# Last batches' routing and loop end in another order, operands of the experts' order in PSUM, conversions in two parts over two steps

## The chip, the cores and the metric

The kernel runs on one core of one Trainium2 chip. The metric is the device time of one execution in microseconds. Three runs of the kernel before took 1173.43, 1176.47 and 1177.87 us, median 1176.47 us.

## The reference, cut to what matters

Three stages follow each other, all in float32: linear attention without a softmax and with a norm per head, a layer of eight experts with a skip, and a gated layer.

```python
# q, k, v: 8 batches, 8 heads, 576 tokens, 64 numbers
kv = einsum('bhsd,bhse->bhde', k, v)
out = einsum('bhsd,bhde->bhse', q, kv)
x = out / sqrt(mean(out * out, -1) + 1e-6) * g_norm      # then 4608 tokens of 512 numbers
...
do_compute = x @ w_skip > 0
e_idx = argmax(x[do_compute] @ w_gate); gate_w = softmax(...)[e_idx]
for e in range(8):                                       # w1 512 x 1024, w2 1024 x 512
    y[mask] = gate_w[mask] * (relu(xc[mask] @ w1[e]) @ w2[e])
x[do_compute] = xc + y
...
h = x @ w_in                                             # 512 x 2048
out = (h * sigmoid(h)) @ w_out                           # 2048 x 512
```

## The kernel before, in words

**Attention** (loop over batches b = 0 to 7 and steps u within each; a batch with odd b has a fifth step for 64 tokens of each of two batches). In every step `attend` multiplies q with the state of two heads' groups into a PSUM tile of the pool `ps_o` (two buffers), ScalarE squares and copies it out into `rows_b[b]`, and VectorE sums the squares (L473, L494). The state of a batch comes from `kv_heads` (k times v, four parts), `kv_copy` (ScalarE) and `kv_state` (two parts, which make the weights `wt`, copied by ScalarE at L450). The dictionary `KV` says in which step which part of which batch's state is made; parts 0 to 3 are `kv_heads`, 4 and 5 are `kv_state`. `early` puts a step's `attend` ahead of the state's parts. `keep_busy` multiplies a unit matrix into a PSUM tile that nobody reads, so that TensorE does not idle.

A pair of batches is then routed: `norm` (the inverse root of the mean square, ScalarE and VectorE), `scale` (GpSimd multiplies the rows, once by g_norm, `grow`, once by the norm, `inv`, at L607), `logits`, `choose`, `count`, `weigh`, `marked`, `ranks` (TensorE, each token's rank within its expert), `own_rank`, `places` and `fill` (TensorE, L783: the lists of tokens of each expert, in the PSUM tile `slots`). `weave` lets several such chains take turns, one VectorE operation at a time. `order_experts` sorts the experts by the number of their tokens in all batches but the last, from the totals `pc` of `sT`; `order_slots` takes the capacities and bases of the sorted experts. SP reads the order into registers (`load_experts`, L559) and issues the loads of the first expert weights.

`store` (SP, L623 and L630) writes a batch's finished rows to the DRAM tile `xs`; `STORES` says in which step. At the end `count` (L1021) is loaded into a register of every engine, and a loop follows that handles experts with more tokens than their capacity; here its count is zero. `gsel` and `gidx` (L959, L964) are the lists sorted by expert. `fetch(0)` gathers the first expert's rows (GpSimd, L967).

Each engine takes its instructions in the order of the program, SP and GpSimd their DMAs too.

**Experts** (steps n = 0 to 63; step n is part f = n % 8 of expert u = n // 8). In a step `first` makes 12 matmuls (L1303), ScalarE and VectorE make the hidden values h and their rest (L1309, L1310), and `second` of the step before makes 9 or 6 (L1355). float32 is multiplied as three products of a rounded part and a rest. So every weight chunk is split: an expert's chunk by ScalarE and VectorE (L187, L188), once a step. A chunk of the gated layer's weights arrives as pairs of integers and is converted by `split`, half a chunk at a time: ScalarE takes the low word (L197), VectorE the high word in five operations (L198 to L210), and later `split_on`, called in every step, has ScalarE write the rounded part (L221), GpSimd multiply and subtract (L222, L223), and, a step later, VectorE add (L218). `at_step` says in which step which conversion is made: 22 in the expert stage, at steps 2, 4 and 6 of each expert and the last at step 55; ten more follow from step 64 on, four operations a step (`split_slowly`).

At an expert's end VectorE adds its result to the rows (L1365, three times), which are stored; `turn` transposes the next expert's rows (TensorE L1204 into a pool `ps_t` of two PSUM tiles, ScalarE L1215, VectorE L1216).

**Gated layer** (from step 64): three groups of 512 tokens in 16 steps each, then six more in pairs.

## Time and profile before

| | us |
|---|---|
| three runs: median (lowest to highest) | 1176.47 (1173.43 to 1177.87) |
| the profiled execution, its own time | 1185.35 |
| its span in the profile | 1183.3 |
| TensorE matmul busy | 1131.6 (96%) |
| TensorE weight load busy | 939.5 (79%) |
| VectorE busy | 595.2 (50%) |
| ScalarE busy | 484.0 (41%) |
| GpSimd busy | 368.8 (31%) |

In the profile PE is TensorE's matmul, PEld its weight load, DVE VectorE, ACT ScalarE, POOL GpSimd and SP the queue that issues most DMAs. Times are from the start of the span. PEclk is the granted TensorE clock as a share of 2.4 GHz. Attention lies in the first 122 us, the experts from about 141 to 405 us, the gated layer behind. "<-" names what ended an idle time; "issue" means that the profile shows nothing that the engine waited for.

### The profile page before, as it was taken

The page shows a single profiled execution, that of the slowest core. Times are in us where ns is not written, and L with a number is a line of the kernel's source. Part 1 is how long each engine was busy: PE and PEld are TensorE (multiplying, and loading weights), DVE is VectorE, ACT ScalarE, POOL GpSimd, SP SyncE. Part 2 cuts the span into 40 slices and gives each one's busy share as a digit, 9 for nine tenths or more (in the row PEclk, how much of TensorE's full clock was granted, in tenths as well). Part 3 has the DMA queues.
Part 4 walks back from the last instruction along what each step waited for, and adds up shares of the span by engine and source line. Part 5 has one row for each costly group of instructions (what it writes and reads, how often), then busy time and mean ns, then how long its engine had stood idle before and what let it go on. Part 6 is the DMA issues. An engine that isn't in the chain of part 4 may idle for free.

```text
span 1183.3 us, 16638 instructions
## 1 busy us (share of the span) xinstructions
PE 1131.6 (96%) x6259; PEld 939.5 (79%) x6259; DVE 595.2 (50%) x1105; ACT 484.0 (41%) x951; POOL 368.8 (31%) x369
## 2 busy tenths in 40 slices
PE   8895699999998999989999999999999999999998
PEld 7785698888886888868878788888888888888886
DVE  2467677788888577624535522355222453223222
ACT  3575354445444443422423444433244432344221
POOL 3679344535444186150063234120043200000000
PEclk9897799999999999999999999999999999999999
DMA  9867656666665433094641376432566322654202
GB/s 341 329 259 296 222 166 210 223 218 210 224 209 200 161 108 115 14 309 155 208 143 54 127 265 216 176 124 91 182 219 221 141 107 104 217 189 170 104 36 71
DMA packets 65265, 211.05 MB, mean 178 GB/s; under 512 B 9840, under 2 KB 24688, under 8 KB 53024
## 3 DMA queue, kind: packets, MB, share of 16 engines
q1 hardware_dynamic: 55760, 189.44, 45.8%
q0 software_dynamic: 8064, 20.48, 5.9%
q8 instruction: 50, 0.82, 0.3%
q10 hardware_dynamic: 1360, 0.05, 0.1%
q14 instruction: 31, 0.25, 0.1%
HBM read 162.67 MB, written 47.27 MB: 177 GB/s over the span
## 4 chain that ended last, share of the span: by engine, by line
PE 87%; DVE 5%; issue 3%; DMA 2%; ACT 2%; POOL 1%; SPq 0%; POOLq 0%; DVEq 0%; ACTq 0%
PE acc L1498 22%; PE acc L1355 19%; PE ph L1303 19%; PE pa L1451 11%; PE pc L1451 6%; PE pb L1451 3%; PE po L456 2%; PE kv L424 1%; PE pt L1204 1%; DVE w L188 1%; POOL x L223 1%; PE kv L426 1%; PE busy L1120 1%; PE G L445 0%; DMA xs<-rows 0%
## 5 line engine op out<-in xcount | busy, mean ns | idle before, releaser
L1355 PE MATMUL acc<-w,h 128*128 128x512 f32 x1128 | 282.4, 397 | 10.7 <-issue 5.5
L1303 PE MATMUL ph<-xT,w 128*128 128x512 f32 (+7 forms) x1344 | 265.8, 347 | 0.8 <-DVE w L188 0.4
L1498 PE MATMUL acc<-entry,h 128*128 128x512 f32 x1152 | 265.1, 392 | 0.0
L1498 PEld LDWEIGHTS acc<-entry,h 128*128 128x128 f32 x1152 | 216.3, 188 | 47.9
L1355 PEld LDWEIGHTS acc<-w,h 128*128 128x128 f32 x1128 | 203.4, 183 | 60.8 <-issue 7.5
L1303 PEld LDWEIGHTS ph<-xT,w 128*128 128x128 f32 x1344 | 225.3, 189 | 30.8 <-DVE w L188 0.7
L1001 POOL DMA_INDIRECT x<-xs,qidx x128 | 128.2, 1002 | 112.8 <-DVE room L1266 48.8
L1451 PE MATMUL pa<-b,entry 128*128 128x512 f32 x576 | 141.8, 393 | 0.0
L1479 DVE TENSOR_TENSOR h<-g,h 128x512 fp32r<-128x512 f32 x96 | 66.5, 693 | 147.8 <-ACT h L1478 145.4
L1451 PEld LDWEIGHTS pa<-b,entry 128*128 128x128 f32 x576 | 108.2, 188 | 24.8
L1478 ACT ACTIVATE h<-g 128x512 fp32r<-128x512 f32 x96 | 60.5, 630 | 146.6 <-PE acc L1498 141.5
L1317 DVE TENSOR_TENSOR h<-sg,h 128x512 fp32r<-128x512 f32 x48 | 34.8, 726 | 119.4 <-ACT h L1316 81.0
L188 DVE TENSOR_TENSOR w<-stg_None,w 128x1024 fp32r<-128x1024 f32 x64 | 80.3, 1256 | 17.3 <-ACT w L187 15.7
L1433 ACT ACTIVATE g<-g 128x512 f32<-128x512 f32 x72 | 45.4, 633 | 103.1 <-DVE g L1431 91.0
L1315 ACT ACTIVATE sg<-ph 128x512 f32<-128x512 f32 x48 | 28.7, 597 | 141.7 <-PE ph L1303 102.4
L222 POOL TENSOR_TENSOR x<-x,x 128x512 f32<-128x512 f32 x32 | 41.6, 1299 | 111.3 <-DVE x L210 106.1
L1451 PE MATMUL pc<-b,entry 128*128 128x512 f32 x288 | 74.3, 393 | 0.0
L1309 ACT ACTIVATE h<-ph 128x304 fp32r<-128x304 f32 (+6 forms) x64 | 28.0, 437 | 109.0 <-PE ph L1303 97.1
L187 ACT ACTIVATE w<-stg_None 128x1024 fp32r<-128x1024 f32 x64 | 67.1, 1049 | 9.8 <-DMA xs<-rows 9.8
L1451 PEld LDWEIGHTS pc<-b,entry 128*128 128x128 f32 x288 | 54.1, 188 | 12.4
L223 POOL TENSOR_TENSOR x<-x,w 128x512 f32<-128x512 f32 x32 | 62.9, 1966 | 0.6 <-ACT w L221 0.6
L1431 DVE TENSOR_TENSOR g<-pc,u 128x512 f32<-128x512 f32 x24 | 16.6, 692 | 73.0 <-PE pc L1451 73.0
(216 smaller groups left out, 1166.8 us busy)
## 6 DMA issues: line engine op xcount, KB each, us to landing
entry<-wa SPq DMA_DIRECT2D x42, 1024.0 KB
stg_None<-in_we_dram SPq DMA_DIRECT2D x64, 512.0 KB
entry<-wb SPq DMA_DIRECT2D x24, 1024.0 KB
stg<-in_wf_dram SPq DMA_DIRECT2D x32, 512.0 KB
xs<-rows SPq DMA_DIRECT2D x8, 1032.0 KB
wb<-w SPq DMA_DIRECT2D x16, 512.0 KB
wa<-parts SPq DMA_DIRECT2D x32, 256.0 KB
k<-in_k_dram SPq DMA_DIRECT2D x7, 1024.0 KB
```

The costliest lines, as they stand in the source:

```text
L187: nc.scalar.activation(w[:, 0, :], t.bitcast(F32), AF.Copy)
L188: nc.vector.tensor_tensor(w[:, 1, :], t.bitcast(F32), w[:, 0, :].bitcast(F32), ALU.subtract)
L222: nc.gpsimd.tensor_tensor(x3, x3, x2, ALU.mult)
L223: nc.gpsimd.tensor_tensor(x1, x1, w[:, 0, :].bitcast(F32), ALU.subtract)
L1001: nc.gpsimd.indirect_dma_start(out=rows_of[u][s][:, a * XQ:(a + 1) * XQ], out_offset=None, in_=xblocks, in_offset=bass.IndirectOffsetOnAxi ...
L1303: nc.tensor.matmul(ph[:, 0:n], w[:, wi, kk * P:(kk + 1) * P], x[:, xi, 0:n], start=(kk == 0 and a == 0), stop=(kk == KD - 1 and a == 2),)
L1355: nc.tensor.matmul(accs[u, s][0:m], h[:, hi, s * P:s * P + m], w[:, wi, DM:2 * DM], start=(f == 0 and a == 0), stop=(last and a == 2),)
L1433: nc.scalar.activation(g, acc, AF.Silu)
L1451: nc.tensor.matmul(p, w[:, wi, kk], x[:, xi, kk], start=(i in FIRST_IN_BANK and kk == 0 and a == 0), stop=(kk == 1 and a == 2), skip_group ...
L1478: nc.scalar.activation(h[:, 0], g, AF.Copy)
L1479: nc.vector.tensor_tensor(h[:, 1], g, h[:, 0].bitcast(F32), ALU.subtract)
L1498: nc.tensor.matmul(acc[ni, s], h[:, hi, s * P:(s + 1) * P], w[:, wi], start=(j == 0 and fi == 0 and a == 0), stop=(last and a == 2),)
```

## The change

What it does:

- `split`: the absolute value of the high word is made by ScalarE instead of VectorE. `split_on`: the subtraction moves from GpSimd to VectorE, next to the addition, a step later.
- `at_step`: 20 conversions in the expert stage instead of 22, at steps 0, 2 and 4 of each expert, the last at step 50. `split_at` does two parts of a conversion in its step and the rest in the next. Twelve follow from step 64 on.
- `KV`: batch 2's products with batch 1's last two steps, its two halves of `kv_state` in batch 2's first step; batches 3 and 4 a step earlier. `early` for batch 1 alone. Three `keep_busy` matmuls behind each half of `kv_state` of batches 1 and 2.
- `STORES`: batches 0 to 5 one by one from batch 4 on.
- Last batches: `sT` is copied a step earlier; `totals` and `ranks` stand behind batch 6's last head; `own_rank` and `places` come with the norm and `order_experts` a step later by itself; `fill` comes behind the last `attend`.
- `order_experts`, `order_slots`, `marked`: operands in PSUM (`key_at`, `put`, `cap_at`, `marks`), with copies to SBUF where another reader needs them.
- `count` is loaded ahead of the last `fill`; `gsel` and `gidx` are made behind the loop, for which `slots` lives longer.
- The last expert's step f = 7: two of the four turns of the next rows ahead of `first`, two behind it.

```diff
@@ split, split_on
         nc.scalar.activation(x3, lo.bitcast(U32), AF.Copy, scale=2.0 ** -52)
-        vec.tensor_scalar(x2.bitcast(I32), hi, 0x7FFFFFFF, None, ALU.bitwise_and)
-        yield
+        nc.scalar.activation(x2, hi.bitcast(F32), AF.Abs)
...
             w, x1, x3 = halfway.pop(0)
+            nc.vector.tensor_tensor(x1, x1, w[:, 0, :].bitcast(F32), ALU.subtract)
             nc.vector.tensor_tensor(w[:, 1, :], x1, x3, ALU.add)
...
             nc.gpsimd.tensor_tensor(x3, x3, x2, ALU.mult)
-            nc.gpsimd.tensor_tensor(x1, x1, w[:, 0, :].bitcast(F32), ALU.subtract)
...
-    NCW = 2 * (NW - NWE)
+    NCW = 2 * (NW - NWE) - 2
...
-        n = (i // 3) * KE + 2 + 2 * (i % 3) if i < NCW - 1 else NE - KE - 1
-        at_step.setdefault(n, []).append((NE + i // 2, i % 2))
+        at_step.setdefault((i // 3) * KE + 2 * (i % 3), []).append((NE + i // 2, i % 2))
...
+    parted = []
+
+    def split_at(n):
+
+        while parted:
+            for _ in parted.pop():
+                pass
+        for task in at_step.get(n, []):
+            g = split(order[nsplit[0]])
+            if task[1] is None:
+                for _ in g:
+                    pass
+            else:
+                for _ in range(2):
+                    next(g)
+                parted.append(g)
             nsplit[0] += 1
             load_ahead()
@@ order_experts, order_slots, routing
             vec.tensor_tensor(
-                at_place, irow[:, 0:E].unsqueeze(2).to_broadcast(sq), place.unsqueeze(1).to_broadcast(sq),
+                put, irow[:, 0:E].unsqueeze(2).to_broadcast(sq), place.unsqueeze(1).to_broadcast(sq),
                 ALU.is_equal,
             )
             yield
-            vec.tensor_tensor(w8, at_place, irow[:, 0:E].unsqueeze(1).to_broadcast(sq), ALU.mult)
+            vec.tensor_copy(at_place, put)
...
-            vec.tensor_copy(ordi, key)
+            vec.tensor_copy(ordi, key_at)
...
-            vec.tensor_scalar(capl, cap, -1.0, float(P - 1), ALU.mult, ALU.add)
+            vec.tensor_copy(cap, cap_at)
+            yield
+            vec.tensor_scalar(capl, cap_at, -1.0, float(P - 1), ALU.mult, ALU.add)
...
+            def mark():
+                vec.tensor_copy(marks[:, 0:T], tok2[:, j0:j0 + T, :])
+                yield
@@ the loop over batches
-        STORES = {(6, 3): (0, 1, 2, 3), (7, 1): (4,), (7, 4): (5,)}
+        STORES = {(4, 1): (0,), (4, 3): (1,), (5, 1): (2,), (5, 3): (3,), (6, 3): (4,), (7, 0): (5,)}
...
-            (2, 0, 0): [(2, i) for i in range(4)], (2, 0, 1): [(2, 4), (2, 5)],
         }
-        for nb in range(3, B):
-            o = {3: 2, 4: 1}.get(nb, 0)
+        for nb in range(2, B):
+            o = {2: 3, 3: 1}.get(nb, 0)
...
                     kv_state(nb, st[nb], part_ - 4)
+                    if nb in (1, 2):
+                        keep_busy(3)
...
-                early = u == 0 and b in (1, 2)
+                early = u == 0 and b == 1
...
                     elif last:
-                        weave(norm(b // 2, 0, R), order_experts(pc))
+                        pc = totals(sT)
+                        route.ranks(ps_kv.tile([P, HP * D], F32, tag="kv", name="rk"))
+                        weave(norm(b // 2, 0, R), chain(route.own_rank, route.places))
...
                         weave(chain(route.so_far, route.choose, route.count, route.marked))
+                        if b == B - 2:
+                            nc.vector.tensor_copy(sT, sumA)
...
                     if u == 1:
-                        weave(chain(route.own_rank, route.places))
-                    if u == 3:
+                        weave(order_experts(pc) if last else chain(route.own_rank, route.places))
+                    if u == 3 and not last:
                         route.fill()
...
-                if b == B - 2 and u == 3:
-                    nc.vector.tensor_copy(sT, sumA)
-                    pc = totals(sT)
-                    route.ranks(ps_kv.tile([P, HP * D], F32, tag="kv", name="rk"))
...
         attend(*prev)
+        route.fill()
         store(B - 2, nc.sync)
...
         weave(chain(r.own_rank, r.places), count_more(pc))
+        count = nc.values_load(ntl[0:1, 0:1], min_val=0, max_val=NT // P)
         r.fill()
@@ the steps
-                for kk in range(KD):
+                for kk in range(KD if u != E - 1 else KD // 2):
                     if at[kk] == f:
                         turn(nxt, kk)
             hs[n] = first(u, f, c)
+            if u == E - 1 and f == at[0]:
+                for kk in range(KD // 2, KD):
+                    turn(nxt, kk)
...
-        split_next(len(at_step.get(n, [])))
+        split_at(n)
```

## Rows read from the trace of the kernel before

**Rows 1.** The page's part 4: the chain that ended last, shares by engine.
```profile
PE 87%; DVE 5%; issue 3%; DMA 2%; ACT 2%; POOL 1%; SPq 0%; POOLq 0%; DVEq 0%; ACTq 0%
```

**Rows 2.** Windows: us, busy us (records) by engine, PEclk, DMA share, GB/s.
```profile
40.00:45.00 5.00, 4.49 (x16) 3.92 (x16) 1.81 (x5) 3.38 (x10) 2.08 (x3) 0.50 1.03 409
115.00:120.00 5.00, 0.00 (x0) 0.00 (x0) 3.99 (x15) 2.96 (x12) 4.55 (x5) 0.50 0.88 317
270.00:280.00 10.00, 10.00 (x57) 8.18 (x55) 9.24 (x16) 5.51 (x9) 3.53 (x2) 1.00 0.54 182
380.00:385.00 5.00, 3.12 (x10) 2.54 (x11) 5.00 (x8) 1.20 (x2) 1.93 (x2) 0.63 0.45 141
385.00:390.00 5.00, 5.00 (x26) 4.53 (x26) 2.62 (x3) 1.33 (x2) 3.44 (x3) 0.69 0.79 253
```

**Rows 3.** Timeline of TensorE, attention's start: start, us, operation [idle before <-releaser].
```profile
19.68 2.43 PE L456 MATMUL po<-wt,q 128*128 128x146 f32 x16 [0.37 <-ACT sc L470]
...
38.42 0.54 PE L445 MATMUL G<-ig,kvT 64*64 64x73 f32 x10 [0.48 <-ACT kvT L430]
...
40.51 4.58 PE L456 MATMUL po<-wt,q 128*128 128x146 f32 x16 [1.03 <-issue]
...
53.81 0.73 PE L445 MATMUL G<-ig,kvT 64*64 64x73 f32 x16 [1.46 <-ACT wt L450]
55.47 0.19 PE L734 MATMUL rk<-Aall,tri 128*128 128x72 bf16 x1 [0.93 <-ACT wt L450]
```

**Rows 4.** The same of TensorE at the end of attention.
```profile
98.12 0.17 PE L504 MATMUL pc<-sT,ones 128*128 128x8 bf16 x1 [2.25 <-DVE sT L926]
...
109.51 0.64 PE L783 MATMUL slots<-cv,roh 128*128 128x24 bf16 x18 [3.93 <-DVE cv L771]
```

**Rows 5.** Timeline of GpSimd at the end of attention.
```profile
87.79 3.47 POOL L607 TENSOR_TENSOR rows<-rows,grow 128x512 f32<-128x512 f32 x3 [1.65 <-ACT rows L469]
...
113.61 3.45 POOL L607 TENSOR_TENSOR rows<-rows,grow 128x512 f32<-128x512 f32 x3 [2.44 <-ACT rows L469]
117.51 4.04 POOL L607 TENSOR_TENSOR rows<-rows,inv 128x512 f32<-128x512 f32 x4 [0.45 <-DVE scratch L596]
```

**Rows 6.** Timeline of VectorE at the end of attention.
```profile
101.53 0.69 DVE L473 TENSOR_REDUCE ssq<-sq 128x8 f32<-128x512 f32 x1 [3.57 <-ACT sq L467]
...
115.33 0.67 DVE L494 TENSOR_REDUCE ssq<-sq 128x8 f32<-128x512 f32 x1
...
121.84 0.28 DVE L695 RECIPROCAL rows<-scratch 128x20 f32<-128x20 f32 x1
```

**Rows 7.** The chain in order of time, around the loop: start, us, what.
```profile
123.20 5.38 DMA xs<-rows
...
129.86 6.08 PE busy L1120 x28
```

**Rows 8.** Timeline of TensorE, from the seventh expert to the first group.
```profile
379.22 0.50 PE L1355 MATMUL acc<-w,h 128*128 128x512 f32 x1 [1.21 <-DVE h L1310]
381.51 1.65 PE L1355 MATMUL acc<-w,h 128*128 128x512 f32 x3 [1.79 <-DVE xe L1365]
...
383.95 2.51 PE L1303 MATMUL ph<-xT,w 128*128 128x256 f32 x10 [0.37 <-DVE w L188]
...
401.88 1.25 PE L1204 MATMUL pt<-ident,sorted 128*128 128x128 f32 x8 [0.98 <-DVE xT L1216]
```

**Rows 9.** Groups by line: count | busy us, mean ns | idle before, releaser.
```profile
L223 POOL TENSOR_TENSOR x<-x,w 128x512 f32<-128x512 f32 x32 | 62.9, 1966 | 0.6 <-ACT w L221 0.6
...
L218 DVE TENSOR_TENSOR w<-x,x 128x512 fp32r<-128x512 f32 x32 | 23.0, 718 | 9.2 <-POOL x L223 9.1
...
L221 ACT ACTIVATE w<-x 128x512 fp32r<-128x512 f32 x32 | 20.2, 632 | 31.4 <-DVE x L206 31.1
...
L198 DVE TENSOR_SCALAR x<-stg 128x512 int32<-128x512 int32 x32 | 14.6, 456 | 0.0
...
L1539 ACT ACT_TABLE_LOAD x1 | 1.3, 1283 | 0.0
```

More of the change, by code (lines that the diff above doesn't have):

```diff
@@ L285, in tile_kernel @@
         ps_o = actx.enter_context(tc.tile_pool(name="ps_o", bufs=2, space=PSUM))
-        ps_s = actx.enter_context(tc.tile_pool(name="ps_s", bufs=1, space=PSUM))
+        ps_s = octx.enter_context(tc.tile_pool(name="ps_s", bufs=1, space=PSUM, side="right"))
         ps_c = actx.enter_context(tc.tile_pool(name="ps_c", bufs=1, space=PSUM))
@@ L871, in state_parts @@
                         kv_copy(nb, st[nb])
-                        if nb + 2 < B:
-                            if nb % 2 == 0:
-                                load(load_rests(nb + 2))
-                            load(load_batch(nb + 2, kv_in))
                 else:
                     kv_state(nb, st[nb], part_ - 4)
+                    if nb in (1, 2):
+                        keep_busy(3)
+                if part_ == 3 and nb + 2 < B:
+                    if nb % 2 == 0:
+                        load(load_rests(nb + 2))
+                    load(load_batch(nb + 2, kv_in))
         route = None
@@ L955, in tile_kernel @@
         weave(chain(r.own_rank, r.places), count_more(pc))
+        count = nc.values_load(ntl[0:1, 0:1], min_val=0, max_val=NT // P)
         r.fill()
-        gsel = ac.tile([P, E, CT, E], F32, name="gsel")
-        nc.vector.tensor_tensor(
-            gsel, slots[:, 0:NS].rearrange("p (e s) -> p s e", e=E).unsqueeze(1).to_broadcast([P, E, CT, E]),
-            at_place.unsqueeze(2).to_broadcast([P, E, CT, E]), ALU.mult,
-        )
-        with nc.allow_low_precision(reason="whole numbers"):
-            nc.vector.tensor_reduce(gidx, gsel.rearrange("p i s e -> p (i s) e"), AX.X, ALU.add)
     def gather(t, idx, n=P):
@@ L1019, in reach @@
         return slot, has, over
-    count = nc.values_load(ntl[0:1, 0:1], min_val=0, max_val=NT // P)
     with ExitStack() as vctx:
@@ L1112, in tile_kernel @@
             vec.tensor_scalar(turn_no, turn_no, 1.0, None, ALU.add)
+    gsel = ac.tile([P, E, CT, E], F32, name="gsel")
+    nc.vector.tensor_tensor(
+        gsel, slots[:, 0:NS].rearrange("p (e s) -> p s e", e=E).unsqueeze(1).to_broadcast([P, E, CT, E]),
+        at_place.unsqueeze(2).to_broadcast([P, E, CT, E]), ALU.mult,
+    )
+    with nc.allow_low_precision(reason="whole numbers"):
+        nc.vector.tensor_reduce(gidx, gsel.rearrange("p i s e -> p (i s) e"), AX.X, ALU.add)
     fetch(0)
```

19 lines of the change are left out of this document (12 added, 7 removed).

## The prediction

> **What bounds the kernel now.** I read the chain of waits first. TensorE carries 87% of it, VectorE 5%, everything else 8% [rows 1], so time is lost where TensorE idles or runs at a low clock, and only what happens there can pay. The windows say where that is: the clock at 0.50 around 40 us, no TensorE work at all from 115 to 120 us, and 0.63 and 0.69 of the clock from 380 to 390 us [rows 2]. Of the two levels (1.2 and 2.4 GHz) 0.50 is the lower one throughout; 0.63 is a mixture. Then I read, engine by engine, what TensorE waited for at these three places.
>
> At the start of attention it waits for ScalarE to copy batch 2's state (0.48 us) and its weights (1.03 us; the row says issue, but the copies of the weights end there), computes 16 matmuls in 4.58 us that took 2.43 us at 19.68 us, and waits twice more for ScalarE's copies of batch 3's weights, 1.46 and 0.93 us [rows 3]. At the end of attention it waits 2.25 us for VectorE's copy sT and 3.93 us for VectorE's cv, with the next heads' matmuls behind both [rows 4]. These waits reach GpSimd: its list of row scalings was caught up at 87.79 us, had no gap until 111.17 us (113.61 less 2.44), then waited 2.44 us for ScalarE's rows of the late heads and 0.45 us for the norm, and ended at 121.55 us [rows 5]. VectorE's last reciprocal ended at 122.12 us [rows 6]. The store of batch 7 follows; its last transfer takes 5.38 us to land, at 128.58 us, and only then does the empty loop let all engines go on [rows 7]. In the expert stage TensorE is nearly always busy, while VectorE is busy 9.24 of 10 us in the fullest window [rows 2]; it overflows once, at the turn from the seventh expert to the eighth, where TensorE waits 1.21, 1.79 and 0.37 us for it [rows 8].
>
> **The change, part by part.**
>
> Batch 2's state. Its key-value products move to batch 1's last two steps, so the copy of the state lies beside other heads. Batch 3's two halves go to two steps with a head's matmuls between. Removed: 0.48 + 1.03 + (4.58 - 2.43) + 1.46 + 0.93 = 6.05 us [rows 3], if the clock stays up. Added: four groups of fillers, 6 records each; 28 such records took 6.08 us at the lower clock [rows 7], so a group is 1.3 us there and 0.65 us at the higher one. In batch 1 one of two groups lies in a wait for ScalarE, 0.7 us; in batch 2 both count, 1.3 us. There the norm's three ScalarE operations now stand ahead of the weights' copies, so TensorE waits for these as before; I take 1.3 us, between the 1.03 and 1.46 us of that wait before. Net 6.05 - 3.3 = 2.7 us. Bounds: 0 if the clock falls all the same, 4 if the fillers hide. The windows behind show TensorE busy up to batch 6's end, so this moves on unchanged.
>
> The stores of batches 0 to 5, now one by one from batch 4 on. I cost them at nothing: SP's queue is in order, and behind a store stand loads of q, issued a batch ahead of their use; rows 0 to 3 have been scaled long before their stores. If that cover is gone, TensorE waits for a load of q, about 3 us for each store of 1 MB that stands ahead.
>
> End of attention. sT is copied earlier and the total moves behind batch 6's last head, so the 2.25 us wait goes; the fill moves behind the loop over batches, so the 3.93 us wait goes [rows 4]. Late next: VectorE's own list. From the idle 3.57 us ahead of 101.53 us on it can start at 97.96 us; before, it took 14.5 us without a gap, to 116.00 us [rows 6]. So it ends by 112.4 us even if nothing gets shorter, and the norm some 1.5 us later, ahead of 114.6 us. The operands in PSUM, three short copies more and some waits for GpSimd less, I cost at nothing, because VectorE is then no longer last: GpSimd is. Its work is unchanged: from 111.17 us another 3.45 and 4.04 us, end 118.66 us instead of 121.55 us [rows 5], 2.89 us earlier, and the store follows it instead of the reciprocal, another 0.57 us. The landing: before, batch 5's and 6's stores and three weight loads were issued shortly ahead of this store; without batch 5's I take 1 us off the 5.38 us, bounds 0 and 2. Together 2.89 + 0.57 + 1.0 = 4.4 us; bounds 2.5 and 5.5.
>
> The load of the loop's count goes ahead of the fill, and gsel behind the loop. The count was not last (the landing was), so no gain. gsel's two small operations, some 0.75 us, now stand ahead of the first gather; the 28 fillers ahead of the transposes, 6.08 us [rows 7], hide them. Without that cover they cost their 0.75 us.
>
> The conversions. VectorE loses the mask (0.456 us) and gains the subtraction, a second operation of the form of L218 (0.718 us): +0.26 us each. GpSimd loses L223, 1.97 us each. ScalarE gains the absolute value, 0.63 us like L221 [rows 9]. VectorE's extra in the expert stage, 20 x 0.26 = 5 us, is paid by two conversions less (six operations of 0.46 to 0.72 us each, some 7 us). What counts is where they stand. The two that leave steps 54 and 55 stood exactly at the turn that overflows; the last are now begun at steps 48 and 50 and over by step 53. Of the 1.21 + 1.79 + 0.37 us [rows 8] and of the clock that fell behind them, (0.37 + 0.31) x 5 = 3.4 us [rows 2], 6.8 us in all, I take 6.0 us, since the three additions of L1365 still stand between the experts; bounds 3 and 6.8.
>
> The last expert's turns, two ahead and two behind the first product: the two PSUM tiles come free during the product, and the 0.98 us wait goes [rows 8], 0.9 us. Steps 64 to 75 take 12 conversions of four parts for 10 of five: TensorE has no gap there, and none comes. Conversion steps at earlier turns may stall a little less or more: 0, within 2 us either way.
>
> Sum: 2.7 + 4.4 + 6.0 + 0.9 = 14.0 us. The profiled execution took 1185.35 us (span 1183.3 us), 8.9 us more than the median of 1176.47 us; the terms are waits of the program's order, which I take to be the same in every run, so they come off the median: **1162.5 us**.
>
> **The rivals.**
>
> Partly hidden: the clock falls in batch 2 all the same (TensorE still idles about 1 us for its weights), and the turn at 380 us keeps half of its stall. For it: the three additions stay, VectorE is as full as before. Against: both conversions left that turn. Gain 0 + 4.4 + 3.0 + 0.9 = 8.3 us: 1168 us.
>
> No change that counts: the store's landing is held by bandwidth, and the stall merely moves to an earlier turn. The end of attention gives its 2.5 us alone: 1174 us. Against it: the waits in rows 4 and 5 come from queue order, not from bandwidth.
>
> Slower: VectorE becomes the bound in the expert stage. Place: the steps after each of the first six turns, where a conversion's first half now meets the three additions L1365 in the same step. From the point at which VectorE is a whole step late, TensorE waits for h and the clock falls: 6.8 us a turn, by the turn at 380 us. Three such turns against all the gains: 1162.5 + 20.4 = 1183 us. For it: 9.24 of 10 us [rows 2]. Against: L223, with which VectorE's operations collide on GpSimd, goes, and a conversion is spread over two steps.
>
> Slower, too: the absolute value is not in the function set that ScalarE holds for Silu. Loading a set takes 1.28 us [rows 9]; two loads are 2.6 us a conversion. ScalarE, busy 5.51 of 10 us [rows 2], has room for them on the mean, but an h that stands behind them comes late; at half of them for each of 20 conversions: 1162.5 + 26 = 1188 us. The Trainium skill, in "ScalarE: Activation LUTs", section "Table sets: the hidden batching unit", says that cheap functions, abs among them, are in every set; no run of before shows an absolute value. By that rule this rival falls away.
>
> **How the numbers follow.** Forecast 0.62, partly hidden 0.23, no change 0.09, VectorE the bound 0.04, the function set 0.02. The range reaches from the upper bounds, 4 + 5.5 + 6.8 + 1 + 2 = 19.3 us, and one more for the spread of the three runs, 1156 us, to the lower ones, 0 + 2.5 + 3 = 5.5 us, and one more, 1172 us. About 0.5% (5.9 us) is what a measurement of this kernel can tell from no change; the forecast and nearly all of the second case lie below 1170.6 us: faster 0.84, same 0.10, slower 0.06.
>
> **What would show it.** Right: no lower clock between 39 and 47 us; no wait of pc for sT and no slots matmuls between the heads; GpSimd's scalings without a gap to their end, and the store right behind them; the loop left some 7 us earlier; full clock at the turn to the eighth expert; no wait between the last transposes; GpSimd's L223 gone; one table load behind the loop. Wrong: a new stretch at the lower clock in attention or at an expert's turn, VectorE without idle time in the expert stage, TensorE waiting for a load behind a store, or for a gather that lands behind the fillers.

## The result, and the profile after

The changed kernel takes 1158.83 us (median of four runs, 1158.19 to 1159.11) against 1175.76 us for the kernel before (now four runs, 1173.43 to 1177.87): ratio 0.9856, 95% interval 0.9836 to 0.9876. The forecast of 1162.5 us was right in sign and nearly in size, but its terms were not all right: two were too small, one was too large, and two losses were missing.

The profiled execution takes 1158.88 us, its span 1157.1 us, 26.2 us less than the span before. Where these come from, by TensorE's first matmul of each stage:

| | before | after | difference |
|---|---|---|---|
| last store lands | 128.58 | 121.40 | -7.2 |
| first expert matmul | 140.57 | 135.51 | -5.1 |
| experts, step 0 to step 64 | 265.2 | 254.8 | -10.4 |
| groups, step 64 to the pairs | 273.1 | 262.4 | -10.7 |
| pairs, to the last matmul | 499.4 | 499.4 | 0 |

The difference in the groups was in no forecast. It belongs to that one execution of the kernel before: ScalarE stood still three times there for 8 to 12 us; the same operation never waits more than 4.2 us in the kernel after. ScalarE's timeline of the kernel before:

```profile
531.16 0.60 ACT L1315 ACTIVATE sg<-ph 128x512 f32<-128x512 f32 x1 [12.13 <-remote]
...
616.95 0.60 ACT L1315 ACTIVATE sg<-ph 128x512 f32<-128x512 f32 x1 [7.86 <-remote]
...
657.83 0.60 ACT L1315 ACTIVATE sg<-ph 128x512 f32<-128x512 f32 x1 [8.09 <-PE ph L1303]
```

The trace doesn't show what released it in the first two. The runs below have such stalls on one chip and not on another, with the kernel after among both, so I don't count them as the change's. No profile of the kernel before is without them.

The chain of waits after: TensorE's share rises from 87 to 90% [rows 1].

```profile
PE 90%; DVE 4%; DMA 3%; ACT 2%; issue 1%; POOL 0%; SPq 0%; DVEq 0%; ACTq 0%
```

The windows after, for four of the five of [rows 2]:

```profile
40.00:45.00 5.00, 4.57 (x70) 3.72 (x68) 1.61 (x5) 3.44 (x11) 4.40 (x5) 1.00 1.03 411
115.00:120.00 5.00, 0.97 (x28) 0.85 (x26) 2.90 (x11) 0.00 (x0) 0.31 (x1) 0.50 1.00 417
...
380.00:385.00 5.00, 5.00 (x35) 4.58 (x35) 3.02 (x4) 2.09 (x5) 0.00 (x0) 1.00 0.68 240
385.00:390.00 5.00, 5.00 (x37) 4.46 (x36) 3.30 (x8) 3.45 (x7) 0.00 (x0) 1.00 0.31 112
```

At 40 us the clock stays at the full 2.4 GHz, and from 380 to 390 us TensorE has no idle time. At the start of attention TensorE's timeline has a filler group and batch 2's first weights (for [rows 3]):

```profile
40.48 0.94 PE L864 MATMUL slots<-ident 128*128 128x128 f32 x6
...
42.33 1.01 PE L474 MATMUL po<-wt,q 128*128 128x146 f32 x6 [0.32 <-ACT wt L468]
```

At the end of attention GpSimd's list runs without a gap from 84.60 to 115.31 us; before it was caught up at 87.79 us and ended at 121.55 us [rows 5]:

```profile
84.60 3.45 POOL L629 TENSOR_TENSOR rows<-rows,grow 128x512 f32<-128x512 f32 x3 [1.53 <-ACT rows L487]
...
111.26 4.05 POOL L629 TENSOR_TENSOR rows<-rows,inv 128x512 f32<-128x512 f32 x4
```

Then the store lands and the loop is left; the chain in order of time, for [rows 7]:

```profile
115.86 5.54 DMA xs<-rows
...
122.51 0.37 DVE gsel L1135
...
124.61 0.28 issue
124.89 5.99 PE busy L1148 x28
```

Before, the fillers started 1.29 us behind the landing; now 3.49 us. That is the first loss, and the first question for the runs. In the expert stage the four kinds of wait of the kernel before are gone, those of [rows 8] and two earlier ones at the transposes among them. TensorE's waits from 140 to 420 us, before the change (what waited <- for what: us in all, times, longest):

```profile
PE pt L1204 <- DVE xT L1216: 3.1, 3, 1.6
PE acc L1355 <- DVE xe L1365: 1.8, 1, 1.8
PE acc L1355 <- DVE h L1310: 1.2, 1, 1.2
PE ph L1303 <- DVE w L188: 0.4, 1, 0.4
```

After, from 130 to 420 us, this is all:

```profile
PE ph L1331 <- ACT xT L1243: 0.3, 1, 0.3
```

The conversions' operations (groups by line, for [rows 9]; L217 is the subtraction, new on VectorE, L198 the absolute value, new on ScalarE):

```profile
L222 POOL TENSOR_TENSOR x<-x,x 128x512 f32<-128x512 f32 x32 | 56.1, 1753 | 96.4 <-DVE x L209 96.2
L217 DVE TENSOR_TENSOR x<-x,w 128x512 f32<-128x512 f32 x32 | 32.8, 1026 | 0.0
...
L198 ACT ACTIVATE x<-stg 128x512 f32<-128x512 f32 x32 | 21.2, 661 | 0.0
...
L1567 ACT ACT_TABLE_LOAD x1 | 1.3, 1283 | 0.0
```

### The profile page after: what moved, and what is told of

It is laid out like the page before. It is cut to its first block, busy times and chain, and to the rows that moved or that the text cites. A ratio compares the mean times of both kernels' runs of the same rounds, so it can differ in the third digit from the quotient of the medians.

```text
span 1157.1 us, 16746 instructions
## 1 busy us (share of the span) xinstructions
PE 1122.7 (97%) x6283; PEld 934.5 (81%) x6283; DVE 601.7 (52%) x1111; ACT 501.8 (43%) x983; POOL 324.2 (28%) x337
## 4 chain that ended last, share of the span: by engine, by line
PE 90%; DVE 4%; DMA 3%; ACT 2%; issue 1%; POOL 0%; SPq 0%; DVEq 0%; ACTq 0%
PE acc L1526 23%; PE acc L1383 21%; PE ph L1331 20%; PE pa L1479 11%; PE pc L1479 6%; PE pb L1479 3%; PE po L474 2%; PE kv L442 1%; PE pt L1232 1%; DMA q<-in_q_dram 1%; DMA v<-in_v_dram 1%; DVE x L217 1%; PE busy L1148 1%; PE kv L444 0%; DVE x L199 0%
## 5 line engine op out<-in xcount | busy, mean ns | idle before, releaser
L1383 PE MATMUL acc<-w,h 128*128 128x512 f32 x1128 | 277.3, 392 | 0.5 <-ACT h L1344 0.5
L1383 PEld LDWEIGHTS acc<-w,h 128*128 128x128 f32 x1128 | 201.0, 181 | 48.0 <-ACT h L1344 1.0
L188 DVE TENSOR_TENSOR w<-stg_None,w 128x1024 fp32r<-128x1024 f32 x64 | 83.9, 1312 | 17.3 <-ACT w L187 17.1
L222 POOL TENSOR_TENSOR x<-x,x 128x512 f32<-128x512 f32 x32 | 56.1, 1753 | 96.4 <-DVE x L209 96.2
L1479 PEld LDWEIGHTS pc<-b,entry 128*128 128x128 f32 x288 | 54.1, 188 | 12.4
L629 POOL TENSOR_TENSOR rows<-rows,grow 128x512 f32<-128x512 f32 x36 | 41.7, 1186 | 31.9 <-ACT rows L487 31.9
```

Of the source, the lines that this page charges most:

```text
L188: nc.vector.tensor_tensor(w[:, 1, :], t.bitcast(F32), w[:, 0, :].bitcast(F32), ALU.subtract)
L222: nc.gpsimd.tensor_tensor(x3, x3, x2, ALU.mult)
L629: nc.gpsimd.tensor_tensor(xv, xv, f.to_broadcast([P, HP, 2, D]), ALU.mult)
L1383: nc.tensor.matmul(accs[u, s][0:m], h[:, hi, s * P:s * P + m], w[:, wi, DM:2 * DM], start=(f == 0 and a == 0), stop=(last and a == 2),)
L1479: nc.tensor.matmul(p, w[:, wi, kk], x[:, xi, kk], start=(i in FIRST_IN_BANK and kk == 0 and a == 0), stop=(kk == 1 and a == 2), skip_group ...
```

## The experiments

e1 to e4 ran on one chip, called the second here, e5 to e12 on another, the third. Which chip the result above comes from isn't on record; I count it as a first. On the second every run was some 20 us longer (the kernel before took 1196.37 us there), nearly all of it in the groups (278 to 283 us, against 262.4 us in the kernel after above), where ScalarE stood still as above. So I compare medians only within a chip (4 to 12 runs each), and otherwise stages, in us, of the one profiled execution of each run:

| run | median us | ratio to before, 95% interval | first expert matmul | experts | groups |
|---|---|---|---|---|---|
| e1 conversions alone | 1186.88 | 0.9921 (0.9893 to 0.9948) | 143.1 | 254.5 | 277.8 |
| e2 attention alone | 1193.20 | 0.9972 (0.9947 to 0.9998) | 141.1 | 264.9 | 282.2 |
| e3 after, loop's code shorter | 1175.70 | 0.9822 (0.9777 to 0.9866) | 134.9 | 255.5 | 282.9 |
| e4 before, loop's code longer | 1197.81 | 1.0002 (0.9975 to 1.0029) | 145.0 | 265.9 | 283.2 |
| e5 after without fillers | 1161.01 | 0.9883 (0.9860 to 0.9906) | 139.8 | 254.9 | 262.5 |
| e6 after, states as before | 1160.59 | 0.9889 (0.9873 to 0.9906) | 135.3 | 254.5 | 262.6 |
| e7 after, fill as before | 1158.71 | 0.9876 (0.9859 to 0.9892) | 134.8 | 255.0 | 262.5 |
| e8 after, stores as before | 1160.97 | 0.9885 (0.9869 to 0.9902) | 141.5 | 255.3 | 262.7 |
| e9 after, again | 1161.24 | 0.9887 (0.9863 to 0.9912) | 135.6 | 254.3 | 262.5 |
| e10 wide fillers, gsel ahead | 1158.41 | 0.9860 (0.9836 to 0.9884) | 133.3 | 255.0 | 262.6 |
| e11 after, schedule as before | 1168.96 | 0.9954 (0.9934 to 0.9974) | 134.7 | 263.5 | 261.3 |
| e12 after, operations as before | 1176.59 | 1.0014 (0.9997 to 1.0031) | 135.0 | 257.6 | 277.5 |

The kernel before took 1196.37 us beside e1 to e4, 1173.92 us beside e5 to e8 and 1174.35 us beside e9 to e12.

### The two halves apart

e1 is the kernel before with the new `split`, `split_on`, `split_at`, `at_step` and the last expert's turns; e2 the kernel after with these as before.

```diff
@@ e1 (the kernel before), the call alone; the rest as in the change
-        split_next(len(at_step.get(n, [])))
+        split_at(n)
```

> The kernel before with the conversions (split, split_on, split_at, at_step) and the last expert's turns of the kernel after, attention and the loop's end as before. Theory: all that the expert stage gained (step 0 to step 64, 265.2 us before, 254.8 us after) belongs to this part, so the stage takes 254 to 256 us, TensorE waits for VectorE at no expert's turn, the first expert matmul stays at 140.6 us, and the median is about 10 us below the kernel before (1165 to 1166.5). Rival: the conversions only look cheap because attention ends elsewhere against the weights' loads; then the stage keeps 3 us or more of the stall at the turn to the eighth expert, 258 us or more.

> The kernel after with the conversions and the last expert's turns of the kernel before. Theory: first expert matmul at 135.5 us (as after, 5.1 us earlier than before), the expert stage as before (265 us, with the waits of 1.2 and 1.8 us at the turn to the eighth expert), median 4.5 to 5.5 us below the kernel before (1170.5 to 1171.5); with the run before, the two parts add up to the 17 us of the change. Rival, the two parts work on each other: they add up to 13 us or less, and the group stage (steps 64 to 112) gains only with both.

In e1 the expert stage takes 254.5 us and TensorE has no wait for VectorE in it; in e2 it takes 264.9 us. TensorE's waits of e2 from 141 to 405 us are those of the kernel before to a tenth:

```profile
PE pt L1215 <- DVE xT L1227: 3.1, 3, 1.6
PE acc L1366 <- DVE xe L1376: 1.8, 1, 1.8
PE acc L1366 <- DVE h L1321: 1.2, 1, 1.2
```

So the gain of the expert stage is the conversions' and the turns' alone. Ahead of that stage both missed what was expected. e1's first expert matmul came at 143.1 us instead of 140.6 us: beside the lower clock at 40 us its profile has a second such stretch, 6.8 us from 54.1 us. e2's came at 141.1 us instead of 135.5 us: its profile began with a low clock from 12.5 to 22.7 us, which put its heads 3.7 to 4.1 us later than those of the kernel after. The medians do not add up: e1's 9.5 us and e2's 3.2 us (4.5 were expected) make 12.7 us, as the rival said (13 us or less), against the 20.7 us of e3, the one run of the kernel after on that chip. But the groups, where the rival saw the difference, take 282.2 us in e2 and 282.9 us in e3, so they gain nothing with both. What the medians on that chip lack stays open.

### TensorE's way out of the loop

What the page can't show, the trace's records of TensorE's sequencer do: the compare-and-branch at the loop's end took 0.31 us before and 3.42 us after. e3 and e4 change only the length of the code that it jumps over.

```diff
@@ e3 (the kernel after)
-            for t in range(NTILE):
-                nc.tensor.matmul(pv, roh[:, t, :], tokb[:, t, :], start=(t == 0), stop=(t == NTILE - 1))
+            for t in range(NTILE - 24):
+                nc.tensor.matmul(pv, roh[:, t, :], tokb[:, t, :], start=(t == 0), stop=(t == NTILE - 25))
@@ e4 (the kernel before)
-            for t in range(NTILE):
+            for t in [*range(24), *range(NTILE)]:
```

> The kernel after, with 24 of the 36 matmuls of the loop over overflowing experts left out; the loop runs zero times here, so no executed instruction changes, only the code of TensorE that the exit jumps over is 48 instructions shorter. That undoes by code length what 24 filler matmuls with 24 weight loads ahead of the loop added. Theory: TensorE's branch out of the loop took 3.42 us in the kernel after and 0.31 us before because its target lay in a block of code that was not yet loaded; here it takes under 0.5 us, the fillers start about 1.3 us after the store's landing instead of 3.5 us, and the first expert matmul comes 1.7 to 2.2 us earlier, at 133.3 to 133.8 us. Rival: the fillers wait for VectorE's gsel and gidx, which now stand behind the loop, or for the bank of slots; then the fillers still start 3.4 us after the landing and the first expert matmul stays at 135.5 us.

> The kernel before with 24 more matmuls in the loop that runs zero times, so the code that the exit jumps over is 48 instructions longer and nothing executed changes. Theory (target of the branch in a block not yet loaded): the branch takes 2 to 3.5 us instead of 0.31 us, and the first expert matmul comes 1 to 2.5 us later than 140.6 us. Rival (VectorE's order or the bank of slots is what delays the kernel after): nothing changes, first expert matmul at 140.5 us. Beside that it shows whether the three stalls of ScalarE in the groups' stage of the kernel before (12.1 us at 519 us and two more) are there in every run: if they are, steps 64 to 112 take 273 us as in the profile of before, if not, about 262 us as in the kernel after.

From the records (landing: end of the last store's transfer in the chain; packet: the first one of 16 KB on the instruction queue q8 behind the branch's start):

| | branch us | landing | first expert matmul, us behind it | packet starts, us into the branch | branch ends, us behind the packet's end |
|---|---|---|---|---|---|
| before | 0.31 | 128.58 | 12.0 | 0.96 | over before |
| after | 3.42 | 121.40 | 14.1 | 0.87 | 1.49 |
| e3 | 0.31 | 122.49 | 12.4 | 0.98 | over before |
| e4 | 3.64 | 130.13 | 14.9 | 0.89 | 1.49 |
| e5 | 0.31 | 127.68 | 12.1 | 1.18 | over before |
| e8 | 6.10 | 130.06 | 11.5 | 3.57 | 1.50 |
| e9 | 3.60 | 121.65 | 14.0 | 0.89 | 1.49 |

The theory holds in both directions: 48 instructions of code that never runs decide over some 2 us. The rival, waits for VectorE, falls: in e3 gsel stands behind the loop as in the kernel after, and the fillers start 1.2 us behind the landing. What TensorE waits for is code. A packet of 16 KB follows the start of the branch in every run, so the packet alone tells nothing: where the branch is short, it is over before the packet starts. Where it is long, in all eight such profiles, it ends 1.49 to 1.51 us behind the packet's end, in e8 too, whose packet starts 3.57 us into the branch. The DMA queues of the kernel after, from 113 to 126 us:

```profile
## 3 DMA queue, kind: packets, MB, share of 16 engines
q1 hardware_dynamic: 570, 2.81, 54.8%
...
q8 instruction: 2, 0.03, 1.0%
```

The Trainium skill says so in "Runtime: NRT & Kernel Launch", section "Instruction fetch mechanics": code comes in blocks of 16 KiB, and a taken branch whose target lies outside the blocks at hand must first fetch its block. e3, e4 and the packets agree. What these runs add is the price beside stores in flight: 3.4 to 3.6 us. e3 kept 0.4 us of the loss, since its transposes waited 1.52 us for VectorE's `goes` (L1177); what that one waited for the trace doesn't name. Its first expert matmul, at 134.9 us, is 1.1 us later than expected, as its landing is. e4's, at 145.0 us, missed the 1 to 2.5 us later that were expected: its heads met stretches of lower clock too, and its landing is 1.6 us later. The groups of e4 took 283.2 us: ScalarE's stalls are not in that one execution alone, but they vary.

### The parts of attention

e5 drops the fillers behind the halves of the states; e6 takes back the table `KV`, with the loads issued beside its parts, `early` and the fillers; e7 puts the fill of batch pair 6 back among the heads; e8 puts the stores back.

```diff
@@ e5
-                    if nb in (1, 2):
-                        keep_busy(3)
@@ e7
-                    if u == 3 and not last:
+                    if u == 3:
                         route.fill()
...
         attend(*prev)
-        route.fill()
@@ e8
-        STORES = {(4, 1): (0,), (4, 3): (1,), (5, 1): (2,), (5, 3): (3,), (6, 3): (4,), (7, 0): (5,)}
+        STORES = {(6, 3): (0, 1, 2, 3), (7, 1): (4,), (7, 4): (5,)}
```

> The kernel after without the four groups of three unit matmuls behind the halves of the states of batches 1 and 2. Two theories on the clock at the start of attention. One: it stays up because batch 2's state now lies beside other heads, and the fillers only cost time; then the clock stays at 1.00 from 38 to 48 us, the po matmul number 192 (64.8 us in the kernel after) comes 1 to 2 us earlier. Two: the fillers hold it up; then a stretch of 3.4 or 6.8 us at the lower clock appears between 28 and 48 us and that matmul comes 1 to 3 us later. Either way TensorE's code ahead of the loop is 48 instructions shorter, as in the kernel before, so by the theory of the branch the branch out of the loop takes under 0.5 us and the first expert matmul follows the store's landing by 12 to 12.5 us (14.1 us in the kernel after, 12.4 us with the loop's code shorter); if the fillers after the loop wait for VectorE, it stays at 14 us.

> The kernel after with the table of the states (KV), the two early steps and the code without fillers of the kernel before; all else as after. Theory: batch 2's weights are waited for again, the clock falls to 0.50 near 40 us for 6.8 us, po matmul number 192 comes near 68.0 us instead of 64.8 us, and GpSimd's list of scalings, which follows the heads, ends 3 us later than the 115.3 us of the kernel after, so the store's landing moves from 121.4 to about 124.5 us. Rival: GpSimd's list is bound by its own work and not by the heads; then po moves by 3 us and the landing by less than 1 us. The branch out of the loop is short here too (no fillers): landing to first expert matmul 12 to 12.5 us.

> The kernel after with the fill of the lists of batch pair 6 back inside the loop over batches, ahead of batch 7's fourth step, as before the change. In the kernel after VectorE's cv ends at 100.4 us, and TensorE would reach the fill at about 97 us. Theory of the prediction (TensorE's wait for cv holds up the last heads, and these GpSimd): TensorE waits 2 to 3.5 us there and GpSimd's scalings get an idle gap ahead of batch 7's rows and end 1.5 to 3 us later than 115.3 us. Rival: GpSimd's list of 30 us has no gap because its own work binds it, and the heads come early enough; then the wait is there and the end of GpSimd's list moves by less than 0.5 us. The branch out of the loop stays at 3 us or more, since the code's length is unchanged.

> The kernel after with the stores of batches 0 to 5 where the kernel before has them (0 to 3 together behind batch 6's fourth step, 4 and 5 in batch 7). Theory: the early stores gain nothing in time: the loads of q, for which TensorE waits 0.25 us at 86 us in the kernel after, come a little earlier (po matmul number 256 at 83.0 to 83.3 us), the last store lands 5.4 to 5.9 us after its issue, and the first expert matmul stays within 0.7 us of 135.5 us. Rival: the stores of the kernel before crowd the end of attention; then the last store takes 7 us or more to land and the first expert matmul comes 1.5 us or more later.

**e5.** The profiles of e5 and e8 both began with the lower clock from 12 us for 13.7 us, which e8 can't have from its edit, so I compare these two. (A po matmul is one of `attend`'s, counted from 0.) Matmul 192 comes at 70.6 us in e5 and 69.6 us in e8: without fillers the heads are 1.1 us later. The last comes at 107.4 and 105.7 us, but there e8's own edit counts, too: it brings its heads forward by 0.4 us against e9. The windows of e5, then of e9 with fillers (behind the busy times of the five engines stands the granted clock):

```profile
32.00:36.00 4.00, 3.51 (x13) 3.20 (x14) 0.21 (x1) 2.05 (x6) 0.00 (x0) 0.57 1.00 412
...
46.00:50.00 4.00, 3.83 (x30) 3.11 (x30) 0.56 (x2) 2.05 (x7) 3.97 (x4) 0.57 1.05 436
```

```profile
32.00:36.00 4.00, 4.00 (x58) 3.43 (x57) 1.38 (x2) 2.20 (x8) 2.33 (x2) 1.00 1.00 416
...
46.00:50.00 4.00, 4.00 (x68) 3.35 (x67) 3.72 (x15) 2.42 (x7) 2.48 (x3) 1.00 0.67 219
```

So the second theory holds: the fillers hold the clock up, and what they save is 1.1 us more than what they take (four groups of 0.94 us, part of it in time in which TensorE would have waited). The 2 us saved at the branch hide the loss in e5's median.

**e6.** po matmul 192 comes at 67.2 us, 2.4 us later than in e9 (64.8 us), matmul 320 2.9 us later, and GpSimd's list and the last store move with them:

```profile
40.63 0.49 PE L474 MATMUL po<-wt,q 128*128 128x146 f32 x2 [1.03 <-issue]
...
51.47 0.73 PE L463 MATMUL G<-ig,kvT 64*64 64x73 f32 x16 [1.46 <-ACT wt L468]
53.13 0.19 PE L760 MATMUL rk<-Aall,tri 128*128 128x72 bf16 x1 [0.93 <-ACT wt L468]
```

```profile
86.92 3.46 POOL L629 TENSOR_TENSOR rows<-rows,grow 128x512 f32<-128x512 f32 x3 [1.69 <-ACT rows L487]
...
113.71 4.04 POOL L629 TENSOR_TENSOR rows<-rows,inv 128x512 f32<-128x512 f32 x4
```

The waits are those of [rows 3] to the hundredth, but the clock did not fall at 40 us; it fell for 3.4 us at 53.7 us. So the waits come every time, and the clock's part varies: the four profiles with the old table (before, e1, e4, e6) have stretches at the lower clock between 28 and 61 us of 6.8, 13.7, 10.2 and 3.4 us in all. The store landed at 124.57 us, as expected; the branch took 0.31 us, and the first expert matmul followed 10.7 us behind the landing, less than the 12 expected.

**e7.** TensorE waits 1.16 us for cv, not 2 to 3.5, and GpSimd's list, 0.4 us earlier from its start, ends at 114.9 us without a gap:

```profile
100.07 0.60 PE L809 MATMUL slots<-cv,roh 128*128 128x24 bf16 x18 [1.16 <-DVE cv L797]
```

```profile
110.85 4.07 POOL L629 TENSOR_TENSOR rows<-rows,inv 128x512 f32<-128x512 f32 x4
```

The rival holds: moving the fill gained nothing. What took most of the 3.93 us wait away is that VectorE makes cv earlier, with the norm: the fill waits for it until 100.07 us here, until 109.51 us in the kernel before [rows 4].

**e8.** The rival holds here, too, for the landing. The heads are 4.4 to 4.8 us later than in e9 by the lower clock at the start (4.8 us already at matmul 32, ahead of the edit); the last store takes 3.6 us longer than in e9 (5.72 us) and lands 8.4 us later:

```profile
120.70 9.36 DMA xs<-rows
```

The branch, too, took 6.10 us and ended 0.3 us behind the landing. The loss and the branch's wait overlap, so the first expert matmul is 5.9 us later than in e9, of which the clock makes some 4.6. An estimate from this one pair of profiles: the early stores are worth 1.3 us in the kernel after (the rival wanted 1.5 us or more), and, by the landing, up to 3.8 us with a short branch.

### Schedule or operations

e11 keeps the new operations and takes the old schedule, e12 the reverse.

```diff
@@ e11
-        at_step.setdefault((i // 3) * KE + 2 * (i % 3), []).append((NE + i // 2, i % 2))
+        n = (i // 3) * KE + 2 + 2 * (i % 3) if i < NCW - 1 else NE - KE - 1
+        at_step.setdefault(n, []).append((NE + i // 2, i % 2))
...
-        split_at(n)
+        split_next(len(at_step.get(n, [])))
@@ e12
-        nc.scalar.activation(x2, hi.bitcast(F32), AF.Abs)
+        vec.tensor_scalar(x2.bitcast(I32), hi, 0x7FFFFFFF, None, ALU.bitwise_and)
+        yield
...
-            nc.vector.tensor_tensor(x1, x1, w[:, 0, :].bitcast(F32), ALU.subtract)
...
+            nc.gpsimd.tensor_tensor(x1, x1, w[:, 0, :].bitcast(F32), ALU.subtract)
...
-    LAST_OPS = 4
+    LAST_OPS = 5
```

> The kernel after with the schedule of the kernel before for the conversions (22 in the expert stage, at steps 2, 4, 6 of each expert and at step 55, each whole in one step), the new operations kept (absolute value by ScalarE, subtraction by VectorE). Theory one, the schedule is what counted (the prediction's reason: the two conversions at the turn to the eighth expert): the stage from first expert matmul to the groups takes 266 to 270 us instead of 259.0 us, with the waits for VectorE at that turn. Theory two, the operations counted (GpSimd no longer has the subtraction with which VectorE's operations collide): the stage stays at 259 to 262 us.

> The kernel after with the operations of the kernel before for the conversions (mask of the sign by VectorE, subtraction by GpSimd), the new schedule kept (20 at steps 0, 2 and 4, in two parts; five instead of four operations a step from step 64 on, so that the twelve conversions behind it end where they did). Theory one, the schedule counted: the expert stage stays at 259 to 261 us. Theory two, the operations counted: 264 us or more, with TensorE waiting for VectorE at the turns. From step 64 on both expect no difference above 1 us, since TensorE has no gap there.

These expectations count the stage to step 65, a step further than the table: by their count e11 takes 267.6 us, e12 261.7 us, the kernel after 259.0 us. In e11 the stall at the turn to the eighth expert is back, with the lower clock from 374.6 us for 6.8 us behind it. Two of TensorE's waits:

```profile
PE acc L1384 <- DVE xe L1394: 2.6, 1, 2.6
PE pt L1233 <- DVE xT L1245: 2.5, 2, 1.5
```

The schedule counted: 9.2 us of the stage (263.5 against 254.3 us in e9), 7.9 us of them at steps 53 to 59, around that turn. The schedule is three things at once, fewer conversions, other steps and two parts; they were not tried apart. The operations are worth 3.3 us with the new schedule (257.6 against 254.3 us), between the two theories, but next to nothing with the old one: the kernel before takes 265.2 us, e11 263.5 us, and the last turns, which e11 keeps new, make 1.4 us of that. And e12 missed behind step 64, where nothing was expected and 15 us were lost (groups 277.5 against 262.5 us). The waits of e12 from 396 to 505 us:

```profile
DVE w L218 <- POOL x L223: 31.1, 12, 5.5
...
PE acc L1384 <- DVE h L1346: 7.1, 10, 0.8
```

VectorE's addition waits for GpSimd's two operations, h stands behind it in VectorE's order, and TensorE waits ten times for h and then falls to the lower clock (0.87 of full speed from 470 to 480 us). So twelve conversions behind step 64 do not fit with the old operations at five operations a step. The old pace of four was not tried with twelve, so the operations and the pace are not told apart there. With the new operations the move costs 1.2 us (groups 262.5 against 261.3 us in e11): at 463 us of the kernel after TensorE waits 0.55 us for h, and the twelve matmuls behind it take 3.31 us instead of 2.72 us.

### Shorter code ahead of the loop

```diff
-            for _ in range(n):
-                nc.tensor.matmul(slots[:, 0:P], ident, ident, start=True, stop=True)
+            for k in (4,) * (n // 4) + (n % 4,) * (n % 4 > 0):
+                out = slots[:, 0:k * P].rearrange("p (o c) -> p o c", o=k)
+                nc.tensor.matmul(out, ident, ident.unsqueeze(1).to_broadcast([P, k, P]), start=True, stop=True)
@@ gsel and gidx ahead of the loop again
```

> The kernel after, unchanged, on the same chip as the next three. All theories: median near 1158.8 us where ScalarE's stalls in the groups' stage don't come, some 20 us more where they do; branch out of the loop 3.4 to 3.6 us; the lower clock from 12 us on (13.7 us long) in some runs, with the heads 4.7 us later.

> The kernel after with two edits that computes the same: the fillers of attention as matmuls of up to 512 columns instead of 128 (the same columns from fewer instructions, so TensorE's code ahead of the loop is over 48 instructions shorter), and gsel and gidx made ahead of the loop as before. Theory (the branch waits for code): branch under 0.5 us, VectorE's two operations hidden by the store's landing, the first gather 1.8 us behind the landing instead of 2.1 us, first expert matmul 11.5 to 12.5 us behind the landing instead of 14.1 us; 1.5 to 2.5 us less than the kernel after in all, 1156.5 to 1157.5 us where that has 1158.8 us. Rival: fillers with fewer weight loads don't hold the clock, a lower stretch comes between 25 and 48 us, and the 2 us are lost again.

e9's branch took 3.60 us, and its profile had no low clock at the start of attention; its runs spread from 1158.50 to 1164.91 us, with the median 2.4 us above the expected one. In e10 the branch takes 0.31 us, and its chain has no piece of VectorE between landing and fillers any more:

```profile
115.21 6.10 DMA xs<-rows
121.31 1.22 issue
122.54 6.09 PE busy L1150 x28
```

The first expert matmul follows the landing by 12.0 us instead of 14.0 us, and the clock stays up from 16 to 104 us. The medians differ by 2.8 us (1158.41 against 1161.24 us); their intervals overlap, so it is the stage, in one profile of each, that shows the 2 us. Its two edits were not tried apart; e3, with a short branch and gsel behind the loop, has 12.4 us there, so gsel's place makes 0.4 us at most.

## Why the prediction was right, step by step

| step of the prediction | forecast us | measured us |
|---|---|---|
| batch 2's state, with fillers | 2.7 | 3.2 |
| stores 0 to 5 early | 0 | 1.3 to 3.8, inside the next line |
| end of attention, to the landing | 4.4 | 4.0 |
| count, gsel, out of the loop | 0 | -2.1 |
| conversions and the last turns | 6.9 | 10.4 |
| steps 64 and on | 0 | -1.2 |
| sum | 14.0 | 14.3 |

The measured sum and ScalarE's stalls in that execution of the kernel before (273.1 less the 261.3 us of e11, 11.8 us) make 26.1 of the 26.2 us of the spans. That forecast and measured sum agree to 0.3 us is luck: 0.5 and 3.5 us too little stand against 0.4, 2.1 and 1.2 us too much. The prediction noted that this execution lay 8.9 us above the median and took its terms off the median; that was sound, since the stalls are no wait of the program's order. The 16.9 us of the medians are 2.6 us more than the sum; on the third chip it is 13.1 us (e9). What makes these differences is open, the sum being from one execution of each kernel.

**Batch 2's state**: right (68.0 to 64.8 us at po matmul 192; e6 gives 2.4 to 3.0 us). The clock's part was argued with too much certainty (3.4 us in e6). The fillers, booked as a cost, are what keeps the clock (e5); a group of them takes 0.94 us at the higher clock, not 0.65 us.

**The stores** failed: "I cost them at nothing" looked only at what stands behind them in SP's queue (there a load of q was late by 0.25 us) and not at what the late stores take from the last one. The term of the landing was wrong as well: it did not fall by 1.0 us (5.54 against 5.38 us). With the stores left late it took 9.36 us (e8).

**End of attention**: right in the engine that ends last, and in size by two errors that nearly cancel. GpSimd's list ends 3.05 us earlier beyond the heads' 3.2 us (forecast 2.89), the store follows its end 1.10 us sooner (forecast 0.57), and the landing gave -0.16 us instead of 1.0. Of the three reasons given for the waits, the move of the fill did nothing (e7); the earlier sT and the new order of VectorE's work were not tried apart. (VectorE's list before the change was read as without a gap; it had one of 0.62 us, which changes nothing here.) The operands in PSUM, costed at nothing because VectorE isn't last, were not tried alone.

**Out of the loop** failed at the step "gsel's two small operations ... the 28 fillers ahead of the transposes ... hide them". The fillers did not start at the loop's end: TensorE's branch, 3.42 us, still waited for code. No row of the kernel before shows the branch, and no term asked what 24 more matmuls do to the code's place.

**The conversions**: the mechanism was right, the size not. By the starts of TensorE's steps in both kernels, the turn to the eighth expert gave 7.6 us (steps 53 to 59; forecast 6.0, at most 6.8), the last turns 1.4 us (forecast 0.9), the turn to the third expert 1.9 us, and the turn to the seventh lost 0.5 us: 10.4 us. The reading that VectorE "overflows once" was wrong: the transposes waited for it at three turns, 1.63, 0.52 and 0.98 us, of which only the last was in the rows read. So "earlier turns: 0" was one mis-sized term, and the turn at 380 us the other. VectorE's extra work was right for the expert stage: the subtraction takes 0.68 us there.

**Steps 64 on**: "TensorE has no gap there, and none comes" failed by 1.2 us, where TensorE waits for h at 463 us. VectorE is full there (5.76 of 6 us busy from 454 to 460 us; the subtraction takes 1.78 us, see below), and the twelve conversions run on to the addition at 464.7 us, past the transposes of the next group's rows (from 460.5 us), with h behind these. In e11 the ten conversions end with the addition at 460.2 us, h stands ahead of the transposes, and TensorE doesn't wait.

**The rivals.** "Partly hidden" was wrong on both points that it named: no lower clock came in batch 2, and nothing is left of the stall at the turn. "No change that counts" did not come: the stall did not move to an earlier turn, though the landing did not get shorter, as it assumed; whether by bandwidth isn't shown. VectorE as the bound did not come. Nor did the function set: the profile has one table load behind the loop, L1567, and 32 absolute values at 0.66 us, as the Trainium skill says in "ScalarE: Activation LUTs", section "Table sets: the hidden batching unit".

## What to carry to other kernels

Fillers and moved work also move the code: behind a branch that is taken once, look at the branch's own time in the trace, and shorten the code in front of it (wider fillers) before blaming the engine whose operations stand there. When a late transfer sets the end, ask of every earlier transfer what it takes from it, not only what waits behind it in its queue. An operation moved off a second engine is worth what stands behind it in order on the first, so try schedule and operations apart: here neither gave the whole gain without the other (e11, e12).

## What the runs showed of the hardware

- A compare-and-branch out of an empty loop takes TensorE 0.31 us or 3.38 to 3.64 us by the length of the code around it alone, and 6.10 us beside the late stores of e8. In the eight profiles with a long branch it ends 1.49 to 1.51 us behind the end of one packet of 16 KB on the instruction queue; that packet starts 0.87 to 0.91 us into the branch, and 3.57 us in e8. What held it back in e8 isn't shown; the stores in flight fit.
- The start of attention has a low clock from 12 us for 10 to 14 us in some executions (e2, e5, e8) and not in others of the same code there (e9 for e2 and e8); it moves all heads by 3.7 to 4.8 us.
- ScalarE's stalls in the groups, three of 8 to 12 us, stand where GpSimd issues 16 gathers in a row. On the second chip all four profiles had them (the groups 15 to 21 us longer than on the third), on the third none of eight, with the same gathers. What holds ScalarE there stays open.

One more shows in the subtraction of the kernel after by its line (shortest, median and longest in ns, first and last start), ahead of 400 us and from 390 to 480 us:

```profile
L217 DVE TENSOR_TENSOR x<-x,w x21: 674/681/686, 149.9 to 399.4; 128x512 f32<-128x512 f32 x21
...
L217 DVE TENSOR_TENSOR x<-x,w x12: 684/1784/1792, 399.4 to 463.9; 128x512 f32<-128x512 f32 x12
```

VectorE's subtraction of two SBUF operands takes 0.68 us, and 1.78 us in the ten cases, all behind step 64, where GpSimd's L222 had begun 0.3 to 0.5 us earlier; in all ten it ends 0.55 to 0.56 us behind L222's end. L222 itself takes 1.6 to 1.7 us in these ten, 1.3 us behind step 64 in the kernel before. The Trainium skill's "SBUF — State Buffer", section "SBUF: two separate sides", says that VectorE and GpSimd share a pair of ports by an exclusive lock, so that one waits for the whole operation of the other; these numbers agree.
